# The second product of a seven-product matrix step adds onto the first one's PSUM bank, and the last 128 output rows leave in one transfer

## The chip, the core and the metric

The kernel runs on one core of a Trainium2 chip. A core has TensorE (PE, with its weight loads listed apart as PEld), VectorE (DVE), ScalarE (ACT), GpSimd (POOL) and SyncE (SP, which here only issues DMA transfers). Each engine works through its own list of instructions in order; waits on semaphores tie the lists together. The metric is the device time of one execution in microseconds (us), as the median of several runs.

## What is computed

Attention with rotary positions (2 batches, 8 heads, 576 tokens, head size 64) gives `x` of 1152 tokens by 512. On it runs a dense mixture of four experts, and this layer alone is touched by the change:

```python
p = domain_probs / (domain_probs.sum(-1, keepdims=True) + 1e-09)
for e in range(E):                       # E = 4
    h = np.maximum(x @ w1[e], 0.0)       # 512 -> 1024
    out += p[:, e:e + 1] * (h @ w2[e])   # 1024 -> 512
```

## The kernel before

Every operand of a matmul is split into a high and a low part in fp32r, so a product is three matmuls: high by high, high by low, low by high. The tokens are cut in two chunks. Chunk 0 (512 tokens of the first batch) goes through the experts while the second batch's attention runs. Chunk 1 (640 tokens) goes through them at the end, alone, and this is where the change lies: class `Moe1`, lines 721 to 850.

**First layer of chunk 1** (`first_layer`, lines 804 to 830). For each expert `e` the 1024 hidden columns are cut into four blocks `i` of 256. A block is a 2 by 2 matrix product done with seven half-size products instead of eight (the Winograd form of Strassen). `product` (line 748) issues one of them: six matmuls of 320 columns into one PSUM bank (lines 758 to 761), then the work on the result. For p1 that is a copy to SBUF on ACT (line 766). p2, p4, p5 and p3 each end a quarter of the hidden layer in `hidden` (line 791): an add in place in the bank on DVE (lines 788, 789), the ReLU into the high part on ACT (line 797), and the low part on DVE (line 799), which is queued behind the next product's DVE work. p6 and p7 and p5 also make the running sums `u` and `v` with one DVE add each. p1's copy is read twice: by p6's add and by p2's add. For expert 0 the order is p1 of all four blocks, p2 of all four blocks, and then p6, p7, p5, p4, p3 block by block. For experts 1 to 3 it is p1, p6, p7, p5, p2, p4, p3 block by block.

**Banks.** There are eight PSUM banks, taken in turn (`bank`, line 740). Expert 0's p1 takes banks 4 to 7; the next four, taken ahead at line 737, are those of its p2.

**Second layer** (`second_layer`, lines 836 to 850). Eight steps `f` of five token tiles `t`, three matmuls of 512 columns each (lines 844 to 846) into five banks. In the last step each tile's bank is mixed into `acc` on DVE (`mix`, line 627; the instruction is at line 633). After the last expert `acc` leaves: tiles 0 to 3 on SP's queue (line 639), tile 4, which holds the last 64 rows of both batches, as two transfers of 64 rows, one on SP's and one on ACT's queue (lines 641 to 644).

**Weights** (`Weights`, lines 481 to 548). `load` issues one DMA of 512 KB on SP; `split` makes the high part on ACT (line 136) and the low part on POOL (line 143); for the first-layer weights of experts 1 to 3 it first makes four sums and differences on DVE (line 538) and splits those too. `next` is a load and a split. In the first layer of experts 1 to 3 it is called after each p4, in the second layer after every second step, the last one behind the mixes.

**Quarters** (lines 646 to 711) prepares the token side of the seven products: sums of quarters of `x` (lines 666, 671) and their split (line 678 on ACT, line 682). Its last five steps stand in the program just before chunk 1's first product, and expert 0's p1 copies stand behind them on ACT.

The order of the instructions is the order of the program; nothing reorders it.

Of the kernel before, what the change touches and what calls it, by code (L numbers as in the profile page):

```python
# [56 lines left out]
def kernel(  # L57
# [17 lines left out]
    nc = tc.nc  # L75
    B, H, S, D = q.shape
    NT, DM = out.shape
    E, _, FF = w1.shape
# [3 lines left out]
    SM = NR * P  # L82
    ST = S - SM
# [7 lines left out]
    NF = FF // P  # L91
    FB = 2

    def f32(ap):
        return ap.bitcast(F32)
# [15 lines left out]
    TH = ctok[1] // 2  # L111
# [34 lines left out]
    class Pair:  # L146


        def __init__(self, b, hp, pool, dst, tail_dst):
            self.b, self.hp, self.nm = b, hp, f"{b}_{hp}"  # L150
            self.pool = pool
            self.dst, self.tail_dst = dst, tail_dst
            self.raw, self.hl, self.tp, self.tl, self.tr = ({} for _ in range(5))
            self.sc, self.mx, self.e, self.et, self.seg = ({} for _ in range(5))
# [394 lines left out]
    class Moe:  # L549
# [77 lines left out]
        def mix(self, e, t, po):  # L627
            p = probs[:, t + self.c * NR, e : e + 1]
            acc = self.acc[t]
            if e == 0:  # L630
                nc.vector.tensor_scalar_mul(acc, po, p)
            else:
                nc.vector.scalar_tensor_tensor(  # L633
                    out=acc, in0=po, scalar=p, in1=acc, op0=ALU.mult, op1=ALU.add
                )
            if e == E - 1:
                if t < NR:
                    rows = out[self.c * S : self.c * S + SM, :].rearrange("(p r) d -> p r d", r=NR)
                    nc.sync.dma_start(out=rows[:, t, :], in_=acc)
                else:  # L640
                    for b in range(B):
                        (nc.sync, nc.scalar)[b].dma_start(
                            out=out[b * S + SM : (b + 1) * S, :], in_=acc[b * ST : (b + 1) * ST]
                        )

    class Quarters:

# [73 lines left out]
    class Moe1(Moe):  # L721
# [3 lines left out]
            p1=("a11", "x00"), p2=("a12", "x10"), p3=("s3", "x11"), p4=("a22", "t4"), p5=("s0", "t1"),  # L725
# [3 lines left out]
        def __init__(self, ctx, quarters):  # L729
            self.c, self.n, self.quarters = 1, ctok[1], quarters  # L730
            tilewise = dict(reuse_waits="tile")
            self.h = ctx.enter_context(tc.tile_pool(name="h1", bufs=1, **tilewise))
            self.pp = ctx.enter_context(tc.tile_pool(name="pm1", bufs=1, space=PSUM, **tilewise))
            self.acc = [
                self.h.tile([P, DM], F32, tag=f"acc{i}", name=f"acc1_{i}") for i in range(self.n // P)
            ]
            self.used, self.ahead = 4, [self.bank(f"p2_{i}", i) for i in range(4)]
            self.x, self.lows = {}, []

        def bank(self, name, i=None):  # L740
# [7 lines left out]
        def product(self, e, i, p):  # L748

            w, x = self.TERMS[p]  # L750
            if w[0] == "a":
                f, d = int(w[1]) - 1, int(w[2]) - 1
                ws = [y[:, 2 * d : 2 * d + 2, f * P : (f + 1) * P] for y in wts.got[1, e, 0, i]]
            else:
                ws = [y[:, int(w[1])] for y in wts.sums[e, i]]
            (wh, wl), (xh, xl) = ws, self.quarters.operand(x)
            o = self.bank(f"{p}{e}_{i}")[:, 0:TH]
            for j in range(2):
                nc.tensor.matmul(o, lhsT=wh[:, j], rhs=xh[:, j], start=(j == 0), stop=False)  # L759
                nc.tensor.matmul(o, lhsT=wh[:, j], rhs=xl[:, j], start=False, stop=False)  # L760
                nc.tensor.matmul(o, lhsT=wl[:, j], rhs=xh[:, j], start=False, stop=(j == 1))  # L761
            x, lows = self.x, self.lows
            self.lows = []
            if p == "p1":
                x["p1", i] = self.temp("p1", e, i, NF // FB)
                nc.scalar.activation(out=x["p1", i], in_=o, func=AF.Copy)
            elif p == "p6":
                x["u", i] = self.temp("u", e, i)
                self.add(x["u", i], o, x["p1", i])
            elif p == "p7":  # L770
                x["v", i] = self.temp("v", e, i)
                self.add(x["v", i], o, x["u", i])
            elif p == "p5":
                self.add(x["u", i], o, x["u", i])
                self.hidden(e, 2 * i + 1, 1, o, x["v", i])
            elif p == "p2":
                self.hidden(e, 2 * i, 0, o, x["p1", i])
            elif p == "p4":
                self.hidden(e, 2 * i + 1, 0, o, x["v", i])
            elif p == "p3":  # L780
                self.hidden(e, 2 * i, 1, o, x["u", i])
            for f in lows:
                f()
# [4 lines left out]
        def add(self, out, o, x):  # L788
            nc.vector.tensor_tensor(out=out, in0=o, in1=x, op=ALU.add)  # L789

        def hidden(self, e, f, t, o, other):

            if f not in self.hh:
                self.hh[f] = [self.h.tile([P, self.n], F32R, tag=f"h{x}{f}", name=f"h{x}1_{e}_{f}") for x in "HL"]
            hi, lo = (x[:, t * TH : (t + 1) * TH] for x in self.hh[f])
            self.add(o, o, other)
            nc.scalar.activation(out=hi, in_=o, func=AF.Relu)  # L797
            self.lows.append(
                lambda: nc.vector.scalar_tensor_tensor(  # L799
                    out=lo, in0=o, scalar=0.0, in1=f32(hi), op0=ALU.max, op1=ALU.subtract  # L800
                )
            )

        def first_layer(self, e):

            nb = NF // FB
            self.hh = {}
            if e == 0:
                for i in range(nb):
                    self.product(e, i, "p1")  # L810
                wts.next()
                for i in range(nb):
                    self.product(e, i, "p2")
                wts.load()
                wts.split()
                wts.load()
            for i in range(nb):
                for p in ("p6", "p7", "p5", "p4", "p3") if e == 0 else ("p1", "p6", "p7", "p5", "p2", "p4", "p3"):
                    self.product(e, i, p)
                    if p == "p4" and e:  # L820
                        wts.next()
                if e == 0:
                    wts.split()
                    if i == 2:
                        wts.split()
                    elif i < 2:
                        wts.load()
            for f in self.lows:
                f()
            self.lows = []  # L830
# [5 lines left out]
        def second_layer(self, e):  # L836
            n = self.n
            po = [self.bank(f"po1_{e}_{t}") for t in range(n // P)]
            for f in range(NF):
                fb, fi = divmod(f, FB)  # L840
                wH, wL = (w[:, fi, :] for w in wts.got[1, e, 1, fb])
                for t in range(n // P):
                    sH, sL = (x[:, t * P : (t + 1) * P] for x in self.hh[f])
                    nc.tensor.matmul(po[t], lhsT=sH, rhs=wH, start=(f == 0), stop=False)  # L844
                    nc.tensor.matmul(po[t], lhsT=sH, rhs=wL, start=False, stop=False)  # L845
                    nc.tensor.matmul(po[t], lhsT=sL, rhs=wH, start=False, stop=(f == NF - 1))  # L846
                    if f == NF - 1:
                        self.mix(e, t, po[t])
                if fi == FB - 1:
                    wts.next()  # L850

    class Agenda:
# [153 lines left out]
    for hp, pr in enumerate(first):  # L1006
# [3 lines left out]
        if hp + 1 < NP:  # L1010
            nx, t = first[hp + 1], TURNS[min(hp, 2)]
# [135 lines left out]
```

## Time and profile before

| | us |
|---|---|
| median of 3 runs | 568.88 |
| lowest and highest run | 568.68, 569.23 |
| profiled execution | 566.62 |
| its span, first to last instruction | 564.8 |

The rows come from the profiled execution; its times count from the start of its span. An execution has 1.8 us outside the span. Chunk 1's four experts fill the span from 348.9 us on.

### The profile page before, as it was taken

To read this page: it belongs to the slowest core of one execution; us is meant where nothing else is said; L and a number is where in the kernel's file an instruction comes from. 1 tells how busy PE (TensorE), PEld (TensorE's weight loads), DVE (VectorE), ACT (ScalarE), POOL (GpSimd) and SP (SyncE) were. 2 spreads that over 40 slices of the span, in tenths; PEclk is the share of its full clock that TensorE was granted. 3 is DMA by queue.
4 is the path that set the end of the run, shared out by engine and by line. 5 is a ranking of instruction groups with operands and counts; after the bars stand their busy time and mean duration, and the time that the engine had idled before them with its cause. 6 is when DMAs were issued, how large, how long until landed. Compare 5 with 4: busy or idle time off the path is not lost. (4 is left out here: it accounts for less than half of the span.)

```text
span 564.8 us, 8507 instructions
## 1 busy us (share of the span) xinstructions
PE 539.7 (96%) x3157; PEld 474.3 (84%) x3157; DVE 324.0 (57%) x587; ACT 281.0 (50%) x561; POOL 339.3 (60%) x240
## 2 busy tenths in 40 slices
PE   4898998999999999999999999999999999999996
PEld 3787887788888888888888888888898899889985
DVE  5588897244363534453344546994587668757702
ACT  5688888555444545555545553453344234324400
POOL 7999984558715871487433487458554655565400
PEclk9899999999999999999999999999999999999999
DMA  5245023352234123432142214522223213222102
GB/s 153 71 117 145 17 51 99 81 173 93 77 113 140 41 76 102 131 97 64 62 128 74 62 52 150 185 76 74 77 77 111 74 39 113 78 76 85 61 1 93
DMA packets 48732, 50.68 MB, mean 90 GB/s; under 512 B 15538, under 2 KB 38322, under 8 KB 48690
## 3 DMA queue, kind: packets, MB, share of 16 engines
q1 hardware_dynamic: 47890, 49.38, 29.0%
q10 hardware_dynamic: 800, 0.75, 0.5%
q8 instruction: 25, 0.41, 0.3%
q14 instruction: 17, 0.14, 0.1%
HBM read 43.34 MB, written 2.36 MB: 81 GB/s over the span
## 5 line engine op out<-in xcount | busy, mean ns | idle before, releaser
L143 POOL TENSOR_TENSOR wl<-wr,wh 128x1024 fp32r<-128x1024 f32 x64 | 154.4, 2413 | 136.0 <-ACT wh L136 136.0
L136 ACT ACTIVATE wh<-wr 128x1024 fp32r<-128x1024 f32 x64 | 67.2, 1052 | 26.5 <-PE po L600 11.9
L300 DVE TENSOR_REDUCE mx<-sc 128x1 f32<-128x576 f32 x72 | 54.2, 753 | 37.7 <-PE sc L289 37.0
L143 POOL TENSOR_TENSOR sl<-sf,sh 128x1024 fp32r<-128x1024 f32 x16 | 38.5, 2407 | 43.0 <-ACT sh L136 43.0
L846 PE MATMUL po<-wh,hL 128*128 128x512 f32 x160 | 62.3, 389 | 0.0
L845 PE MATMUL po<-wl,hH 128*128 128x512 f32 x160 | 62.3, 389 | 0.0
L844 PE MATMUL po<-wh,hH 128*128 128x512 f32 x160 | 62.3, 389 | 0.0
L308 ACT ACTIVATE e<-sc,mx 128x576 f32<-128x576 f32 x72 | 53.3, 740 | 17.7 <-DVE mx L300 16.7
L584 DVE SCALAR_TENSOR_TENSOR hL<-ph,hH 128x512 fp32r<-128x512 f32 x32 | 22.1, 692 | 60.1 <-ACT hH L583 60.1
L598 PE MATMUL po<-wh,hH 128*128 128x512 f32 x128 | 52.3, 409 | 0.0
L136 ACT ACTIVATE sh<-sf 128x1024 fp32r<-128x1024 f32 x16 | 17.0, 1060 | 70.5 <-DVE sf L538 64.9
L623 PE MATMUL ph<-xH,wh 128*128 128x512 f32 x128 | 51.5, 402 | 0.0
L624 PE MATMUL ph<-xL,wh 128*128 128x512 f32 x128 | 50.1, 392 | 0.4 <-POOL xL L424 0.4
L343 DVE TENSOR_TENSOR ptL<-pp,ptH 128x512 fp32r<-128x512 f32 x64 | 44.0, 687 | 11.1 <-ACT ptH L339 10.3
L339 ACT ACTIVATE ptH<-pp 128x512 fp32r<-128x512 f32 x64 | 38.1, 595 | 24.6 <-PE x L372 17.3
L600 PE MATMUL po<-wh,hL 128*128 128x512 f32 x128 | 50.3, 393 | 0.0
L625 PE MATMUL ph<-xH,wl 128*128 128x512 f32 x128 | 50.1, 392 | 0.0
L599 PE MATMUL po<-wl,hH 128*128 128x512 f32 x128 | 50.0, 391 | 0.0
L797 ACT ACTIVATE hH<-p 128x320 fp32r<-128x320 f32 x64 | 27.1, 436 | 40.3 <-DVE p L789 40.3
L322 PE MATMUL pp<-ident,e 128*128 128x128 f32 x288 | 44.7, 279 | 2.1 <-DVE ptL L343 1.1
L538 DVE TENSOR_TENSOR sf<-wr 128x256 f32<-128x256 f32 x30 | 32.7, 1129 | 16.9 <-DMA wr<-in_moe_w_dram 16.9
L322 PEld LDWEIGHTS pp<-ident,e 128*128 128x128 f32 x288 | 34.2, 142 | 8.1 <-ACT e L308 2.4
(171 smaller groups left out, 1373.4 us busy)
## 6 DMA issues: line engine op xcount, KB each, us to landing
wr<-in_moe_w_dram SPq DMA_DIRECT2D x68, 512.0 KB, 3.6
k2T<-kT SPq DMA_DIRECT2D x14, 288.0 KB, 4.1
rawv<-in_v_dram SPq DMA_DIRECT2D x16, 128.0 KB, 3.0
out_dram<-acc SPq DMA_DIRECT2D x8, 256.0 KB, 4.0
rawk<-in_k_dram SPq DMA_DIRECT2D x7, 256.0 KB, 3.8
rawq<-in_q_dram SPq DMA_DIRECT2D x7, 256.0 KB, 3.1
rawv<-in_v_dram SPq DMA_DIRECT2D x16, 32.0 KB, 2.3
tabs<-in_rope_dram ACTq DMA_DIRECT2D x1, 320.0 KB, 3.4
```

The lines of the kernel that those rows point to most:

```text
L136: nc.scalar.activation(out=hi, in_=src, func=AF.Copy)
L143: eng_l.tensor_tensor(out=lo, in0=src, in1=f32(hi), op=ALU.subtract)
L300: nc.vector.tensor_reduce(out=mx, in_=self.sc[u][:, :, 0:HALF], op=ALU.max, axis=AX.XY, negate=True)
L308: nc.scalar.activation(out=e.rearrange("p (i c) -> p i c", i=2), in_=self.sc.pop(u)[:, :, 0:HALF], func=AF.Exp, bias=self.mx.pop(u), accum ...
L322: nc.tensor.transpose(pp[:, c * P : (c + 1) * P], self.e[u][:, c * P : (c + 1) * P], ident)
L598: nc.tensor.matmul(po[t], lhsT=sH, rhs=wH, start=(f == 0), stop=False)
L600: nc.tensor.matmul(po[t], lhsT=sL, rhs=wH, start=False, stop=(f == NF - 1))
L623: nc.tensor.matmul(o, lhsT=wH[:, kt], rhs=xh, start=(kt == 0), stop=False)
L624: nc.tensor.matmul(o, lhsT=wH[:, kt], rhs=xl, start=False, stop=False)
L844: nc.tensor.matmul(po[t], lhsT=sH, rhs=wH, start=(f == 0), stop=False)
L845: nc.tensor.matmul(po[t], lhsT=sH, rhs=wL, start=False, stop=False)
L846: nc.tensor.matmul(po[t], lhsT=sL, rhs=wH, start=False, stop=(f == NF - 1))
```

## The change

p2's six matmuls accumulate onto p1's bank, after p1's copy has been read from it by ACT, so p2's sum is complete in PSUM and its add on DVE is gone; the copy stays for p6. A block uses six banks instead of seven, and the four banks taken ahead go to the first four products behind p2. The last `next` of a second layer moves to behind the first p1 of the next expert. Tile 4 of the output leaves in one transfer of 128 rows on ACT's queue.

```diff
@@ mix
-                    for b in range(B):
-                        (nc.sync, nc.scalar)[b].dma_start(
-                            out=out[b * S + SM : (b + 1) * S, :], in_=acc[b * ST : (b + 1) * ST]
-                        )
+                    nc.scalar.dma_start(out=out.rearrange("(b s) d -> b s d", s=S)[:, SM:S, :], in_=acc)
@@ Moe1.__init__
-            self.used, self.ahead = 4, [self.bank(f"p2_{i}", i) for i in range(4)]
+            self.used, self.ahead = 4, [self.bank(f"p6_{i}", i) for i in range(4)]
@@ product
-            o = self.bank(f"{p}{e}_{i}")[:, 0:TH]
+            onto = p == "p2"
+            o = self.x.pop(("p1 sum", i)) if onto else self.bank(f"{p}{e}_{i}")[:, 0:TH]
+            group = dict(skip_group_check=True) if p in ("p1", "p2") else {}
             for j in range(2):
-                nc.tensor.matmul(o, lhsT=wh[:, j], rhs=xh[:, j], start=(j == 0), stop=False)
-                nc.tensor.matmul(o, lhsT=wh[:, j], rhs=xl[:, j], start=False, stop=False)
-                nc.tensor.matmul(o, lhsT=wl[:, j], rhs=xh[:, j], start=False, stop=(j == 1))
+                nc.tensor.matmul(o, lhsT=wh[:, j], rhs=xh[:, j], start=(j == 0 and not onto), stop=False, **group)
+                nc.tensor.matmul(o, lhsT=wh[:, j], rhs=xl[:, j], start=False, stop=False, **group)
+                nc.tensor.matmul(o, lhsT=wl[:, j], rhs=xh[:, j], start=False, stop=(j == 1), **group)
             if p == "p1":
+                x["p1 sum", i] = o
                 x["p1", i] = self.temp("p1", e, i, NF // FB)
                 nc.scalar.activation(out=x["p1", i], in_=o, func=AF.Copy)
...
             elif p == "p2":
-                self.hidden(e, 2 * i, 0, o, x["p1", i])
+                self.hidden(e, 2 * i, 0, o)
@@ hidden
-        def hidden(self, e, f, t, o, other):
+        def hidden(self, e, f, t, o, other=None):
...
-            self.add(o, o, other)
+            if other is not None:
+                self.add(o, o, other)
@@ first_layer
-                    if p == "p4" and e:
+                    if e and (p == "p4" or i == 0 and p == "p1"):
                         wts.next()
@@ second_layer
-                if fi == FB - 1:
+                if fi == FB - 1 and f < NF - 1:
                     wts.next()
```

## Rows read from the trace of the kernel before

**Rows 1.** Page, part 1: busy us, share of the span, instructions of each engine.

```profile
PE 539.7 (96%) x3157; PEld 474.3 (84%) x3157; DVE 324.0 (57%) x587; ACT 281.0 (50%) x561; POOL 339.3 (60%) x240
```

**Rows 2.** Windows by stage: length, busy us (instructions) per engine, PEclk, DMA share, GB/s.

```profile
348.00:377.00 29.00, 27.09 (x174) 25.43 (x173) 27.34 (x59) 13.11 (x26) 15.30 (x9) 1.00 0.47 162
377.00:404.20 27.20, 27.20 (x121) 22.51 (x121) 15.51 (x26) 10.07 (x13) 21.25 (x9) 1.00 0.24 78
404.20:429.00 24.80, 24.80 (x170) 24.79 (x169) 19.34 (x45) 11.79 (x23) 12.38 (x6) 1.00 0.28 87
...
533.00:561.00 28.00, 26.95 (x119) 21.96 (x117) 5.37 (x10) 1.71 (x3) 2.40 (x1) 1.00 0.08 28
```

**Rows 3.** Timeline of PE, expert 0's first layer: start, us, instruction, [idle before <-releaser].

```profile
352.29 0.31 PE L761 MATMUL p<-xH,wl 128*128 128x320 f32 x1
...
356.18 0.31 PE L761 MATMUL p<-xH,wl 128*128 128x320 f32 x1
356.83 0.41 PE L759 MATMUL p<-tH,sh 128*128 128x320 f32 x1 [0.34 <-ACT p L766]
...
364.38 0.42 PE L759 MATMUL p<-t1H,sh 128*128 128x320 f32 x1 [0.49 <-DVE hL L799]
...
369.84 0.41 PE L759 MATMUL p<-t1H,sh 128*128 128x320 f32 x1 [0.78 <-DVE hL L799]
...
376.98 0.39 PE L844 MATMUL po<-wh,hH 128*128 128x512 f32 x1
```

**Rows 4.** Timeline of ACT around the first copies of p1.

```profile
352.37 0.81 ACT L678 ACTIVATE tH<-s 128x320 fp32r<-128x320 f32 x2
355.84 0.47 ACT L678 ACTIVATE tH<-s 128x320 fp32r<-128x320 f32 x1 [2.65 <-DVE s L671]
356.34 1.43 ACT L766 ACTIVATE p<-p 128x320 f32<-128x320 f32 x4
```

**Rows 5.** Timeline of DVE in the same layer: two of p2's adds, p6's first add.

```profile
358.40 0.89 DVE L789 TENSOR_TENSOR p<-p,p 128x320 f32<-128x320 f32 x2
...
363.45 0.48 DVE L789 TENSOR_TENSOR u<-p,p 128x320 f32<-128x320 f32 x1
```

**Rows 6.** Timeline of ACT in expert 1's first layer: copies of p1, blocks 0 and 1.

```profile
408.57 0.42 ACT L766 ACTIVATE p<-p 128x320 f32<-128x320 f32 x1
...
414.14 0.44 ACT L766 ACTIVATE p<-p 128x320 f32<-128x320 f32 x1
```

**Rows 7.** Timeline of the end: last matmul, the last transfer on ACT's queue.

```profile
559.56 0.39 PE L846 MATMUL po<-wh,hL 128*128 128x512 f32 x1
...
560.77 0.55 ACTq L642 DMA_DIRECT2D out_dram<-acc  x1
```

**Rows 8.** Line 642, its two transfers of 128 KB: issue to landing.

```profile
DMA to landing us min/median/max: 2.4/2.7/3.0
```

**Rows 9.** Windows of the end, columns as in rows 2.

```profile
558.90:559.60 0.70, 0.70 (x5) 0.55 (x3) 0.70 (x2) 0.00 (x0) 0.00 (x0) 1.00 0.98 366
...
563.20:563.50 0.30, 0.00 (x0) 0.00 (x0) 0.00 (x0) 0.00 (x0) 0.00 (x0) 1.00 0.07 27
```

**Rows 10.** Tile `probs`, line 122: the transfer that loads the same 128 rows' probabilities.

```profile
L122 SPq DMA_DIRECT2D probs<-in_moe_domain_probs_dram x1: 647/647/647, 19.8 to 19.8; - x1
```

**Rows 11.** Window while that transfer moves, columns as in rows 2.

```profile
21.40:21.50 0.10, 0.10 (x3) 0.10 (x1) 0.10 (x1) 0.10 (x2) 0.10 (x1) 0.98 0.19 5
```

**Rows 12.** Windows at three changes of the granted clock, columns as in rows 2.

```profile
17.50:18.00 0.50, 0.11 (x2) 0.00 (x0) 0.00 (x0) 0.50 (x2) 0.50 (x1) 0.99 0.25 57
18.00:18.50 0.50, 0.00 (x0) 0.00 (x0) 0.00 (x0) 0.50 (x3) 0.50 (x2) 0.50 0.51 160
...
21.00:21.50 0.50, 0.50 (x4) 0.50 (x3) 0.47 (x2) 0.50 (x2) 0.41 (x2) 0.60 0.07 2
...
564.00:564.20 0.20, 0.00 (x0) 0.00 (x0) 0.00 (x0) 0.00 (x0) 0.00 (x0) 0.81 0.00 0
```

**Rows 13.** Timeline of PE around the first of these falls.

```profile
16.62 0.53 PE L238 MATMUL tpq<-identr,hlq 128*128 128x128 f32 x4 [0.80 <-POOL hlq L143]
...
18.56 0.85 PE L289 MATMUL sc<-kT,qT 128*128 128x288 f32 x2 [0.95 <-ACT e L308]
```

## The prediction, made before the changed kernel was run

> **What bounds the kernel now.** I read the page first: PE is busy for 96% of the span [rows 1], so only its idle time and what lies before its first and behind its last matmul can move the end. Then the windows by stage [rows 2]. From 377 us on PE has no gap: the second layer of expert 0 fills 27.20 of 27.20 us, the first layer of expert 1 fills 24.80 of 24.80, and experts 2 and 3 look the same, up to the last matmul at 559.56 us [rows 7]. Work taken off DVE there (19.34 busy of 24.80) is worth nothing. The one stage with gaps is expert 0's first layer: 27.09 of 29.00 us. Its price per matmul I take from expert 1, where nothing waits: 168 matmuls (4 blocks, 7 products, 6 matmuls) in 24.8 us, 0.1476 us each. Expert 0's 168 should so take 24.8 us. They start at 352.29 - 23 x 0.1476 = 348.9 and end at 376.98 [rows 3], 28.1 us: 3.3 us of gaps, in front of the products behind p2, with ACT's p1 copy and DVE's low parts as releasers. So the timeline of PE there is the next view, and those of ACT and DVE beside it [rows 4, 5]. Last comes the tail: from 559.56 us to the end of the span 5.3 us pass, in which only output leaves.
>
> **Part 1, p2 onto p1's bank, expert 0.** What goes: p2's four adds, two of them in 0.89 us [rows 5], some 1.7 us of DVE. What comes: p2's first matmul, which in the kernel before went into a bank of its own, has to wait until ACT has copied p1's sum out of the bank that it now adds to. That copy is late. ACT works in order; ahead of the four copies stands a split of Quarters that waits 2.65 us for DVE until 355.84, and the copies run from 356.34 on, four in 1.43 us [rows 4]. Nothing in the change touches what they wait for. PE is done with p1's 24 matmuls at 352.4 and went straight on into p2, up to 356.18 [rows 3]; now it finds nothing to do until the first copy is out. That very event has a row: p6's first matmul takes the bank of the first p1 before, was released by the copy and started at 356.83 [rows 3]. So p2 starts at 356.83, and queued behind it on PE are 4 + 20 products, 144 matmuls: 144 x 0.1476 = 21.25 us, with 0.1 us for the first matmul behind a wait (0.41 instead of 0.31 us), to 378.2 us. That stands against 376.98: **+1.2 us**, if all later gaps are gone.
>
> Are they? They came from banks which DVE released late: p5's first matmul of the second block waited for a low part until 364.38, that of the third until 369.84 [rows 3]. DVE began p6's adds at 363.45, 5.7 us behind p6's end near 357.7. In the changed kernel p2 ends at 360.4, its ReLUs and low parts by about 361, the weight sums follow, and p6's first add comes at about 362.7: DVE is 0.7 us earlier, PE 3.6 us later. Walking the eight banks with 0.4 us per DVE instruction and 0.88 us per product, the tightest place, p5 of the third block at 370.9 on the bank of p3 of the first, finds it free at 369.1. I take 0 for later gaps; if DVE is late by what it was, 0.5 to 1 us comes on top.
>
> **Part 2, what the wait does to the clock.** The wait leaves PE without work from 352.6 to 356.8, some 4.1 us; the longest gap that PE has in the trace once its work has begun is 0.95 us [rows 13]. Two rows show the granted clock fall from 2.4 to 1.2 GHz: at 18.0 us, after PE had worked only in pieces with gaps of 0.80 and 0.95 us [rows 12, 13], and at 564.1, 4.2 us after the end of the last matmul at 559.95 [rows 7, 12]. At 18.0 far less idleness was enough than here, so I expect a fall during this wait or just behind it. Price: the first fall lasted to about 21.4 (the half-microsecond to 21.5 has 0.60), with PE at work again from 18.56: 2.8 us at half the clock [rows 12, 13], of which half is lost, **+1.4 us**. The ends are 0 (no fall) and 2.8 us (the low clock lasts twice as long). PE paces this stage afterwards, so the loss goes into the end in full.
>
> The Trainium skill, page "TensorE: Matmul & The Clock Gate", section "Why this matters for your kernels", speaks against this part: gaps between bursts of matmuls send the clock back to the low level. By it the sum is the one with the fall, without it the second case below. The trace agrees as far as it goes: it has a fall 4.2 us behind the last matmul [rows 7, 12].
>
> **Part 3, experts 1 to 3.** Twelve adds go, PE has no gap that they could close: 0. Does the new wait bite? p2 is fifth in its block, so it wants p1's copy 4 x 0.885 = 3.5 us behind the block's start. In expert 1's block 0 (start 404.2) the copy ran at 408.57 [rows 6], too late for a p2 at 407.7. But it ran there behind the splits that the change now puts behind it: p1 ends at 405.3, so the copy ends by 405.8. Block 1's copy ended at 414.58 [rows 6] where p2 will start at 404.2 + 6.2 + 3.5 = 413.9; p6's first add, which waited for block 0's copy, starts some 2.4 us earlier now, so DVE and ACT come to block 1 without that lag, and the copy follows p1's end at 411.5. Cost 0, with 0.7 us for each block after the first as the other end, if the lag stays.
>
> The moved `next`: its load keeps its place among SP's loads, as nothing else is on that queue between; its four sums keep theirs on DVE, as p1 has no DVE work; on ACT two splits now stand behind p1's copy, and with them POOL's two. Their product is block 3 of the next expert's first layer, wanted 18.5 us later: 0. With six banks a block, p7 of the next block takes the bank of p2: it starts at 7.9 us in block time, p2's low part ends near 6.4. Cost 0 with 1.5 us of cover.
>
> **Part 4, the last transfer.** Before, 256 KB left as two transfers issued at 560.77 [rows 7], which landed 2.4 and 3.0 us later [rows 8]. Their data were out by 563.2 [rows 9], and the first could not start before about 561.9, 1.1 us after issue, with the four earlier tiles ahead of it: 1.3 us for the data. The new one has the form of line 122 [rows 10]: the last 64 rows of two batches as an outer dimension of two. While that one moved, the DMA share was 0.19 and 5 GB/s [rows 11], at most 3 of 16 engines' time, where output of 128 plain rows has 0.98 and 366 GB/s [rows 9]; it is also the only transfer here without a landing shown. So I expect that the outer two is spread over two engines. An engine's pace from [rows 9] is 366 / (0.98 x 16) = 23.3 GB/s. 262,144 bytes on two engines take 5.6 us, on three 3.7, on sixteen 0.7. I take two, since there are two outer rows: 5.6 instead of 1.3 us, **+4.3 us**, nothing behind it to hide it. The other end is all sixteen, where the tail saves what the SP transfer was later than ACT's, up to 0.6 us.
>
> The Trainium skill, page "DMA: Bandwidth & Descriptors", section "Why a DMA increments its semaphore by 16 and not by 1", says that a transfer uses the largest number of engines up to 16 which divides the slowest dimension of both its patterns. That gives 2 here and 16 for the two transfers of 64 rows. The row of line 122 agrees in direction (0.19 of the engines). Without the rule the sum would be that of the third case below.
>
> **Sum.** 1.2 + 1.4 + 4.3 = 6.9 us. On the profiled execution: span 564.8 to 571.7, execution 566.62 to 573.5. The median of the runs is 2.3 us above the profiled one; on it the forecast is 568.88 + 6.9 = **575.8 us**.
>
> **The rivals.**
> - *The clock holds* over the wait: 568.88 + 5.5 = 574.4. For it: the gap before the fall at the end was as long, so the fall might come too late to matter. Against: the fall at 18.0. Chance 0.2.
> - *The transfer spreads over sixteen engines* as the others do: 575.8 - 4.3 - 0.3 = 571.2, or 569.8 if the clock holds too. For it: line 122 is a load of 2 KB and tells little of a store of 256 KB. Chance 0.12.
> - *The freed DVE pays*, the other side: the copies of p1 are out before PE wants p2, all 3.3 us of gaps close and the tail is neutral: 565.6. It decides from copies that end by 352.4 on; each microsecond later costs one, and at 355.7 nothing is left. The copies' row ends 356.8 to 357.8. Chance 0.04, in which a slow tail would leave 569.9, about the time of now.
> - *The lag in experts 1 to 3 stays*: 0.7 us for each of 9 blocks, up to 6.3 us: 577 to 582. For it: block 1's row. Against: both causes of the lag are removed. Chance 0.08.
>
> **How the numbers follow.** The forecast has 0.56. Its own bounds: part 1 +1.0 to +2.2, the clock 0.6 to 2.8, the tail 3.7 to 4.5, so about 574.2 to 578.4. With the held clock (down to 573.4) and the lower part of the lag (to 578.8) the range is 573.2 to 578.8 and leaves the sixteen engines, the freed DVE and the upper half of the lag outside, 0.2. About 0.2% is what a measurement of this kernel can tell from no change, 567.7 to 570.0. Faster: 0.03. Same: 0.04, from part of the sixteen engines with the clock held and of the freed DVE. Slower: 0.93.
>
> **What would show it.** Part 1: a PE gap of about 4 us in front of line 759's first p2, released by ACT's p1 copy, the second layer's start at 378 to 380, and no gap by DVE's low parts behind it. Part 2: PEclk of 0.50 within 355 to 362 us. Part 3: first layers of 24.8 us without idle PE. Part 4: a landing of some 7 us, and a DMA share near 0.12 to 0.19 in the last microseconds. The forecast is wrong if ACT's copies run before 355 us, or if the last transfer lands within 3 us.

## The result: 1.4% slower, and where the time went

The changed kernel takes 577.25 us (median of 6 runs, 575.05 to 578.14) against 568.84 us for the kernel before in the same runs: ratio 1.0142, 95% interval 1.0122 to 1.0163, so 6.9 to 9.3 us more. The profiled execution took 577.79 us, its span is 576.0 us. The page of after, which answers to [rows 1], with the slices of the granted clock:

```profile
span 576.0 us, 8485 instructions
...
PE 543.6 (94%) x3157; PEld 478.5 (83%) x3157; DVE 319.0 (55%) x571; ACT 280.7 (49%) x561; POOL 338.9 (59%) x240
...
PEclk9999999999999999999999999899999999999997
```

The 16 adds are gone from DVE (571 instead of 587 instructions). PE's busy time rose although it does the same matmuls: part of them ran at a lower clock. Windows by stage are the next view (columns as in [rows 2]): expert 0's first layer, then everything up to the last matmul, then the tail. First the kernel before, cut at its own stage limits, then after.

```profile
348.92:376.98 28.06, 26.16 (x169) 24.66 (x168) 26.47 (x58) 13.09 (x26) 14.38 (x8) 1.00 0.45 156
376.98:559.95 182.97, 182.97 (x986) 163.81 (x984) 113.70 (x209) 62.63 (x103) 94.03 (x39) 1.00 0.22 72
559.95:564.83 4.88, 0.00 (x1) 0.00 (x0) 0.79 (x2) 0.00 (x0) 0.00 (x0) 0.93 0.59 190
```

```profile
350.92:382.67 31.75, 27.57 (x169) 27.30 (x168) 27.56 (x59) 15.58 (x28) 15.81 (x9) 0.89 0.50 155
382.67:565.64 182.97, 182.97 (x986) 163.80 (x984) 106.46 (x191) 59.81 (x100) 92.34 (x39) 1.00 0.22 69
565.64:576.00 10.36, 0.00 (x1) 0.00 (x0) 0.79 (x2) 0.00 (x0) 0.00 (x0) 0.69 0.26 90
```

Three things are to be seen. The middle, 183 us with three of the four experts, is the same to the hundredth, with 7 us less of DVE in it. Expert 0's first layer is 3.7 us longer, the tail 5.5 us. Together 9.2 us; the spans differ by 11.2. The other 2.0 us lie ahead of 348.92 and 350.92, where both programs are the same: this start varies from run to run, and in the traces it goes with how long the granted clock is low in the opening. In the four traces in which chunk 1 begins by 349.2 us the low level ends by 21.6 us (in before at 21.4 [rows 12]); in the nine others it lasts past 22 us. That this is the whole 2.0 us is argued, not shown. The same two matmuls of both runs on the timeline of PE, before at the high level and then after at the low one:

```profile
14.91 0.53 PE L289 MATMUL sc<-kT,qT 128*128 128x288 f32 x2 [0.42 <-ACT e L308]
```

```profile
14.88 0.85 PE L289 MATMUL sc<-kT,qT 128*128 128x288 f32 x2 [0.41 <-ACT e L308]
```

In all the kernels below chunk 1 began between 348.9 and 351.3 us. So stages are compared by their length, and times by their ratio.

**Expert 0's first layer.** Timelines of PE and of ACT in after, answering to [rows 3, 4]:

```profile
354.28 0.31 PE L760 MATMUL p<-xH,wl 128*128 128x320 f32 x1
358.78 0.64 PE L758 MATMUL p<-xH,wh 128*128 128x320 f32 x1 [4.18 <-ACT p L766]
359.21 0.47 PE L759 MATMUL p<-xL,wh 128*128 128x320 f32 x1
...
382.67 0.39 PE L845 MATMUL po<-wh,hH 128*128 128x512 f32 x1
```

```profile
357.79 0.47 ACT L675 ACTIVATE tH<-s 128x320 fp32r<-128x320 f32 x1 [2.61 <-DVE s L668]
358.29 1.42 ACT L766 ACTIVATE p<-p 128x320 f32<-128x320 f32 x4
```

p2's first matmul waits 4.18 us for p1's copy, which stands on ACT behind the split that waits for DVE. That is the only gap that PE has from here to the end; the gaps in front of the later products [rows 3] are gone. But behind the wait a matmul takes 0.47 us instead of 0.31. Windows behind the wait:

```profile
358.78:364.75 5.97, 5.97 (x22) 5.97 (x23) 2.90 (x8) 3.19 (x7) 2.38 (x1) 0.50 0.40 150
364.75:382.67 17.92, 17.92 (x123) 17.92 (x123) 16.95 (x42) 9.65 (x16) 8.72 (x4) 1.00 0.31 89
```

The granted clock is at 0.50 for 5.97 us of PE's work. In that time PE did 22 matmuls; at 0.1476 us each they take 3.2 us at full clock. So some 2.7 us went to the clock and 1.0 us to the wait itself.

**The tail.** The last transfer's issue, SP's last wait before and in after, and three windows of after while the transfer is alone:

```profile
566.47 1.12 ACTq L641 DMA_DIRECT2D out_dram<-acc  x1
```

```profile
SPq L1142 <- DMA out_dram<-acc: 2.4, 1, 2.4
```

```profile
SPq L1143 <- DMA out_dram<-acc: 8.8, 1, 8.8
```

```profile
569.00:570.00 1.00, 0.00 (x0) 0.00 (x0) 0.00 (x0) 0.00 (x0) 0.00 (x0) 0.78 0.15 27
570.00:571.00 1.00, 0.00 (x0) 0.00 (x0) 0.00 (x0) 0.00 (x0) 0.00 (x0) 0.50 0.11 43
571.00:572.00 1.00, 0.00 (x0) 0.00 (x0) 0.00 (x0) 0.00 (x0) 0.00 (x0) 0.50 0.14 55
```

SP waited 8.8 us at the end for the output, 2.4 us before the change. The mean busy share of the sixteen DMA engines is 0.11 to 0.15, as if two of sixteen worked (0.125), with 27 GB/s at first and 43 to 55 later. The packets in the trace say the same: from 568 us on, two packets of 2 KB are under way at a time. The Trainium skill, page "DMA: Bandwidth & Descriptors", section "Why a DMA increments its semaphore by 16 and not by 1", says that a transfer runs on the largest number of engines, up to 16, that divides the slowest dimension of both its patterns, here two. The trace agrees with its two packets at a time.

### The profile page after: what moved, and what is told of

Its sections match the earlier page's. It is cut to its first block, busy times and chain, and to the rows that moved or that the text cites. A ratio compares the mean times of both kernels' runs of the same rounds, so it can differ in the third digit from the quotient of the medians.

```text
span 576.0 us, 8485 instructions
## 1 busy us (share of the span) xinstructions
PE 543.6 (94%) x3157; PEld 478.5 (83%) x3157; DVE 319.0 (55%) x571; ACT 280.7 (49%) x561; POOL 338.9 (59%) x240
```

## The experiments

"First layer" is expert 0's, from its first matmul to the second layer's first; "tail" runs from the end of the last matmul to the end of the span. Both are from the profiled execution of each kernel. Each ratio is against the kernel before as run beside that kernel, with medians of 568.00 to 568.84 us; e5 and e11 rest on two runs each. The stretch between them was 182.97 us in every one of these kernels.

| kernel | first layer | tail | median, us | ratio to before (95%) |
|---|---|---|---|---|
| before | 28.06 | 4.88 | 568.84 | |
| after | 31.75 | 10.36 | 577.25 | 1.0142 (1.0122 to 1.0163) |
| e1_two_transfers | 31.36 | 4.70 | 571.92 | 1.0067 (1.0042 to 1.0092) |
| e2_tail_alone | 28.07 | 10.38 | 572.93 | 1.0094 (1.0062 to 1.0126) |
| e3_filled_wait | 29.13 | 4.90 | 568.72 | 1.0014 (0.9997 to 1.0032) |
| e4_copies_first | 28.03 | 4.69 | 568.29 | 1.0001 (0.9986 to 1.0016) |
| e5_one_on_sp | 28.08 | 9.71 | 572.68 | 1.0083 (1.0053 to 1.0113) |
| e6_two_on_act | 28.08 | 5.36 | 569.11 | 1.0011 (0.9997 to 1.0026) |
| e7_experts_1_to_3 | 28.07 | 4.86 | 568.60 | 1.0003 (0.9992 to 1.0015) |
| e9_ve_relieved | 28.20 | 4.89 | 568.90 | 1.0011 (0.9998 to 1.0024) |
| e10_sums_behind | 27.53 | 4.87 | 568.09 | 1.0000 (0.9985 to 1.0015) |
| e11_column_halves | 28.07 | 10.74 | 573.43 | 1.0097 (1.0059 to 1.0136) |
| e12_sums_ahead | 26.34 | 4.90 | 566.90 | 0.9963 (0.9949 to 0.9976) |

**The two parts of the change, each alone.** e1 is the changed kernel with the two transfers of before; e2 is the kernel before with the one transfer.

```diff
  e1, against after
-                    nc.scalar.dma_start(out=out.rearrange("(b s) d -> b s d", s=S)[:, SM:S, :], in_=acc)
+                    for b in range(B):
+                        (nc.sync, nc.scalar)[b].dma_start(
+                            out=out[b * S + SM : (b + 1) * S, :], in_=acc[b * ST : (b + 1) * ST]
+                        )
  e2, against before: the same lines the other way round
```

> The changed kernel with the last 128 rows sent as before, 64 rows on each of two queues. Theory (the two parts of the change cost separately: 5.5 us in the tail, some 3 us by p2's wait and the clock behind it): 571.7 us, 2.9 above the kernel before; the tail from the last matmul to the end of the span is 4.9 us again; the gap of 4.2 us in front of p2 stays. Rival (the transfer is slow because of something earlier in the changed kernel, not by its form): the tail stays near 10 us and the time near 577.

> The kernel before with nothing but the one transfer of 128 rows on ScalarE's queue. Theory (its form puts it on two of the engines): 568.8 + 5.5 = 574.3 us, tail some 10 us, PE's work as before. Rival (a transfer of 256 KB on one queue costs as others do): 568 to 569 us.

Measured: e1 has the tail of before and the long first layer, e2 the reverse; 1.0067 and 1.0094 make 1.016, the changed kernel has 1.0142. So the parts add up within their intervals. e2's 572.93 us lie 1.4 under what was expected, while its tail of 10.38 us is what was expected; the runs' starts vary by as much.

**What makes the transfer slow: queue, bytes or form?** e5 puts the one transfer on SP's queue, e6 puts both transfers of 64 rows on ACT's, e11 sends two transfers of the new form, each with half of the columns, on the two queues.

```diff
  e5, against e2
-                    nc.scalar.dma_start(
+                    nc.sync.dma_start(
  e6, against before
-                        (nc.sync, nc.scalar)[b].dma_start(
+                        nc.scalar.dma_start(
  e11, against e2
+                    for i in range(2):
+                        a, z = i * DM // 2, (i + 1) * DM // 2
+                        (nc.sync, nc.scalar)[i].dma_start(
+                            out=out.rearrange("(b s) d -> b s d", s=S)[:, SM:S, a:z], in_=acc[:, a:z]
+                        )
```

> The kernel before with the one transfer of 128 rows on SyncE's queue in place of ScalarE's. Theory (the outer dimension of two puts it on two engines, whatever the queue): tail 10 us or more, DMA share near 0.13 while it moves, 573 to 575 us. Rival (ScalarE's queue is what is slow): tail 5 us, 568.8 us.

> The kernel before with both transfers of 64 rows on ScalarE's queue. Theory (the form decides, not the queue or the number of bytes on it): tail within 0.7 us of the kernel before, 568.5 to 569.5 us. Rival (256 KB on one queue behind each other are slow): tail 8 us or more.

> The kernel before with the last 128 rows as two transfers that each have the outer dimension of two and half of the columns, one on SyncE's and one on ScalarE's queue. Theory (an outer dimension of two means two engines, the same two for each transfer): tail about 10 us as with one transfer, DMA share near 0.13, 573 us. Rival (each transfer gets two engines of its own): the data take half as long, tail near 7.5 us, DMA share near 0.25.

Measured: on SP the tail is 9.71 us, a little under the 10 us expected, so 0.7 us of it go with the queue. Two of the old form behind each other on ACT cost 0.5 us, not 5. Windows during the transfer in e5 and then in e11, where two transfers of the new form run at once:

```profile
566.00:567.00 1.00, 0.00 (x0) 0.00 (x0) 0.00 (x0) 0.00 (x0) 0.00 (x0) 0.50 0.13 51
```

```profile
568.00:569.00 1.00, 0.00 (x0) 0.00 (x0) 0.00 (x0) 0.00 (x0) 0.00 (x0) 0.50 0.14 47
569.00:570.00 1.00, 0.00 (x0) 0.00 (x0) 0.00 (x0) 0.00 (x0) 0.00 (x0) 0.50 0.13 47
```

Two such transfers on two queues together still have 0.13 to 0.14 of the engines and two packets under way at a time: they share the same two. So the form decides, and splitting such a transfer over queues doesn't help.

**Is the clock a cost of its own?** e3 is e1 with work for PE during the wait.

```diff
  e3, against e1
+        def fill(self, e, i):
+            wh = wts.got[1, e, 0, i][0][:, 0:2, 0:P]
+            xh = self.quarters.operand("x00")[0]
+            o = self.ahead[i][:, 0:TH]
+            for j in range(6):
+                nc.tensor.matmul(o, lhsT=wh[:, j % 2], rhs=xh[:, j % 2], start=(j == 0), stop=(j == 5))
...
+                for i in range(nb):
+                    self.fill(e, i)
                 for i in range(nb):
                     self.product(e, i, "p2")
```

> As e1, and in front of expert 0's first p2 stand 24 matmuls of 320 columns onto the four banks that p6 to p4 of the first block take later; nobody reads their sums. p2 still waits for p1's copy, but PE works meanwhile. Theory (the wait costs 1.2 us by itself and the rest of the 3 us is the clock that falls over it): PEclk stays at 1.0 over this layer, 570.0 us, 1.7 below e1. Rival (the clock's fall is paid by slack that DVE would have taken anyway): the time of e1, 571.7 us.

Timeline of PE and two windows of e3 during and behind the wait:

```profile
353.82 4.06 PE L813 MATMUL p<-xH,wh 128*128 128x320 f32 x24
358.21 0.42 PE L761 MATMUL p<-xH,wh 128*128 128x320 f32 x1 [0.33 <-ACT p L769]
```

```profile
355.00:358.00 3.00, 2.88 (x18) 2.61 (x18) 2.97 (x5) 0.76 (x2) 1.31 (x1) 1.00 0.97 364
358.00:361.00 3.00, 2.79 (x19) 2.79 (x20) 1.83 (x5) 2.19 (x6) 0.00 (x0) 1.00 0.41 126
```

p2 still starts when the copy is out, but at clock 1.00. The first layer takes 29.13 us, 2.2 less than e1, where the low clock covered 5.1 us of PE's work: that is the clock's price. What is left over before, 1.07 us, is the wait's. The time fell further than expected, to 568.72 us instead of 570.0; of the 3.2 us between the medians of e1 and e3 the layer accounts for 2.2, the rest is not resolved. Twenty-four useless matmuls make the kernel faster than nothing in their place.

**Experts 1 to 3.** e7 is e1 with the accumulation in these experts only.

```diff
  e7, against e1
-            onto = p == "p2"
+            onto = p == "p2" and e > 0
-                self.hidden(e, 2 * i, 0, o)
+                self.hidden(e, 2 * i, 0, o, None if onto else x["p1", i])
```

> As e1, but only experts 1 to 3 add p2 onto p1's bank; expert 0 has its own banks and the add for p2, as in the kernel before. Theory (PE has no gap in experts 1 to 3 either way, and p1's copy there comes before PE wants p2): 568.7 us, no PE gap in these experts, the first layer of expert 0 takes 28.1 us again. Rival (the copies come late there too, up to 0.7 us a block): 571 to 575 us.

Measured: no difference to the kernel before (0.9992 to 1.0015), and 182.97 us of gapless PE. Twelve fewer DVE adds are worth nothing there, and accumulating onto a bank that ACT has read costs nothing either.

**If the copy came in time, would the freed DVE pay?** e4 is e1 with the last steps of Quarters behind p1's products, so that ACT has the copies first.

```diff
  e4, against e1
                     self.product(e, i, "p1")
+                for _ in range(5):
+                    quarter_step()
                 wts.next()
...
-        for _ in range(5):
-            quarter_step()
```

> As e1, with the last five steps of the quarters moved behind expert 0's four p1 products, so that on ScalarE p1's copies stand ahead of the split that waits for VectorE. Theory (p2's cost is the late copy, nothing in the accumulation itself): no gap of 4 us, PEclk 1.0, the first layer of expert 0 ends some 2 us earlier than in the kernel before, 566.5 us. Rival (adding onto a bank that another engine has just read is slow, or VectorE's late start holds the layer anyway): 568.8 us or more.

Half of this came: p2 waits 0.36 us and the clock stays at 1.00. But the layer takes 28.03 us, as before, not 26. PE, DVE and POOL in e4:

```profile
354.50 0.42 PE L761 MATMUL p<-xH,wh 128*128 128x320 f32 x1 [0.36 <-ACT p L769]
...
365.90 0.42 PE L761 MATMUL p<-t1H,sh 128*128 128x320 f32 x1 [0.48 <-DVE hL L803]
371.35 0.42 PE L761 MATMUL p<-t1H,sh 128*128 128x320 f32 x1 [0.79 <-DVE hL L803]
```

```profile
361.52 1.29 DVE L803 SCALAR_TENSOR_TENSOR hL<-p,hH 128x320 fp32r<-128x320 f32 x3 [1.51 <-ACT hH L801]
362.72 1.52 DVE L538 TENSOR_TENSOR sf<-wr 128x256 f32<-128x256 f32 x2
...
364.96 0.48 DVE L792 TENSOR_TENSOR u<-p,p 128x320 f32<-128x320 f32 x1
```

```profile
361.24 2.39 POOL L143 TENSOR_TENSOR sl<-sf,sh 128x1024 fp32r<-128x1024 f32 x1 [4.78 <-ACT sh L136]
```

p6's first add comes 364.96 - 350.46 = 14.5 us after the layer's start; before the change it was 363.45 - 348.92 = 14.5 [rows 5]. The 1.6 us of adds that were taken out turned into waiting: DVE waits 1.51 us instead of 0.70 for p2's ReLUs, which stand on ACT behind a split, and a pair of sums takes 1.52 us instead of 0.75. The wait, one of the adds and the same pair in the kernel before, on DVE, and then POOL:

```profile
359.99 0.49 DVE L799 SCALAR_TENSOR_TENSOR hL<-p,hH 128x320 fp32r<-128x320 f32 x1 [0.70 <-ACT hH L797]
360.40 0.49 DVE L789 TENSOR_TENSOR p<-p,p 128x320 f32<-128x320 f32 x1
...
361.99 0.75 DVE L538 TENSOR_TENSOR sf<-wr 128x256 f32<-128x256 f32 x2
```

```profile
359.71 2.40 POOL L143 TENSOR_TENSOR sl<-sf,sh 128x1024 fp32r<-128x1024 f32 x1 [4.77 <-ACT sh L136]
```

There the sums begin as POOL's subtraction ends (362.1), and take 0.75 us; the add, with one operand in PSUM, took its usual 0.49 us beside POOL. In e4 the sums begin in the middle of POOL's subtraction: the first of the pair alone takes 1.19 us and ends 0.3 us behind POOL's instruction, the second takes its usual 0.41 us. So DVE's sums stand still while POOL works, and the adds of before had filled time in which the sums would have stood still anyway.

e9 was made before I had seen this: it moves the second block's sums to POOL and the splits behind p2.

```diff
  e9, against e4
-                (nc.vector if e or fb else nc.gpsimd).tensor_tensor(out=x[:, o], in0=p, in1=q, op=op)
+                (nc.vector if e or fb > 1 else nc.gpsimd).tensor_tensor(out=x[:, o], in0=p, in1=q, op=op)
-                wts.next()
                 for i in range(nb):
                     self.product(e, i, "p2")
+                wts.next()
```

> As e4, and two things that take the load off VectorE before p6: the weight sums of the second block of expert 0 run on GpSimd instead of VectorE, and the load and split that stood between p1 and p2 stands behind p2, so that p2's ReLUs on ScalarE don't stand behind a split. Theory (in e4 the freed adds of VectorE turned into waiting for these ReLUs, and VectorE holds the layer): p6's first add comes 3 to 4 us earlier against the layer's start than the 14.5 us of the kernel before, the layer takes 26 to 27 us instead of 28.1, and the time is 567 to 567.5 us. Rival (the low part of the second block's sums, later on GpSimd, takes the place of VectorE): a wait for it in front of p6 of the second block, 28 us, 568.7 us.

Neither theory had it. The layer takes 28.20 us and p6's first add comes at 363.69 - 349.02 = 14.7 us. DVE and POOL of e9:

```profile
356.24 2.91 DVE L682 TENSOR_TENSOR tL<-s,tH 128x320 fp32r<-128x320 f32 x3
359.07 1.27 DVE L803 SCALAR_TENSOR_TENSOR hL<-p,hH 128x320 fp32r<-128x320 f32 x3
360.27 2.71 DVE L538 TENSOR_TENSOR sf<-wr 128x256 f32<-128x256 f32 x2
```

```profile
354.97 1.95 POOL L538 TENSOR_TENSOR sf<-wr 128x256 f32<-128x256 f32 x2
356.89 0.97 POOL L538 TENSOR_TENSOR sf<-sf,wr 128x256 f32<-128x256 f32 x1
357.94 0.86 POOL L538 TENSOR_TENSOR sf<-wr,sf 128x256 f32<-128x256 f32 x1
359.97 2.39 POOL L143 TENSOR_TENSOR sl<-sf,sh 128x1024 fp32r<-128x1024 f32 x1 [1.17 <-ACT sh L136]
```

With POOL at work three low parts of the quarters (`tL`) take 2.91 us (1.29 in e4 and e10, where POOL rests), and a pair of sums 2.71 us instead of 0.75. What POOL took over DVE lost again. The Trainium skill, page "SBUF — State Buffer", section "Who interferes with whom", says that a VectorE instruction with two inputs in SBUF contends with a GpSimd instruction that reads SBUF, and one with at most one such input does not. The traces agree on both: sums and low parts of `s` against the adds from PSUM.

e10 and e12 test this by order alone. e10 keeps all sums on DVE and puts them ahead of POOL's subtraction, behind p2; e12 puts them ahead of p2's work as well, with the splits still behind p2's ReLUs.

```diff
  e10, against e4
-                wts.next()
                 for i in range(nb):
                     self.product(e, i, "p2")
+                wts.next()
  e12, against e10: the sums split off from the splits
+                wts.load()
+                wts.ahead(2)       # the sums of the next two blocks
                 for i in range(nb):
                     self.product(e, i, "p2")
-                wts.next()
+                wts.split()
```

> As e4, but the weight sums and splits of expert 0's second and third block stand together behind p2's four products; all sums stay on VectorE. Theory (in e4 and e9 VectorE's sums of the third block stood still under GpSimd's 2.4 us subtraction for the second block, in which the kernel before had its adds; here both sums come ahead of that subtraction): p6's first add comes 12 to 13 us after the layer's start instead of 14.5, no sum takes over 0.6 us by more than one instruction, and the next that is late is the second block's low part from GpSimd, 1.5 to 2 us in front of p6 of the second block; the layer takes 27 to 27.7 us. Rival (VectorE's own amount of work sets 14.5 us): 14 us or more, layer 28 us.

> As e10, but VectorE makes the sums of expert 0's second and third block ahead of p2's work, while the splits of these sums on ScalarE and GpSimd stay behind p2's ReLUs. Theory (the layer is held by the chain of VectorE's sums, ScalarE's high part and GpSimd's low part in front of p6 of the second block): GpSimd's low part comes 1.4 us earlier against the layer's start, the gap of 1.97 us of e10 shrinks to about 0.6 us, the layer takes 26.1 to 26.5 us instead of the 28.1 us of the kernel before, and the time is 566.3 us against 568.2, about 0.3% less. Rival (VectorE, with its low parts later, holds the banks): a gap in front of p5 of the second block as in the kernel before, layer 27.5 us or more.

PE, DVE and POOL of e10, then of e12:

```profile
364.57 0.42 PE L763 MATMUL p<-tH,sl 128*128 128x320 f32 x1 [1.97 <-POOL sl L143]
...
362.21 0.48 DVE L792 TENSOR_TENSOR u<-p,p 128x320 f32<-128x320 f32 x1
...
362.06 4.82 POOL L143 TENSOR_TENSOR sl<-sf,sh 128x1024 fp32r<-128x1024 f32 x2 [5.97 <-ACT sh L136]
```

```profile
364.25 0.41 PE L772 MATMUL p<-tH,sl 128*128 128x320 f32 x1 [0.41 <-POOL sl L143]
...
360.39 0.75 DVE L551 TENSOR_TENSOR sf<-wr 128x256 f32<-128x256 f32 x2
...
363.05 0.48 DVE L801 TENSOR_TENSOR u<-p,p 128x320 f32<-128x320 f32 x1
...
361.70 4.86 POOL L143 TENSOR_TENSOR sl<-sf,sh 128x1024 fp32r<-128x1024 f32 x2 [4.78 <-ACT sh L136]
```

In e10 p6's first add comes 362.21 - 350.06 = 12.2 us after the layer's start, the sums run unhindered, and PE now waits once, 1.97 us, for POOL's low part: 27.53 us, within the expected bounds, though too little for the time to show it. In e12 that low part starts 361.70 - 350.90 = 10.8 us after the layer's start instead of 12.0, PE waits 0.41 us, and the layer takes 26.34 us. e12 is faster than both kernels: 0.9963 (0.9949 to 0.9976) of the kernel before. It has the accumulation, the two transfers of before, the copies first and the sums first. No run has the new order without the accumulation, so how its gain divides between the two is not shown.

## Why the prediction held, step by step

Forecast 575.8 us in a range of 573.2 to 578.8; measured 577.25, and 8.1 us by the ratio where the sum was 6.9.

- **What bounds the kernel:** right. The stretch behind expert 0's first layer did not move, 182.97 us in all kernels.
- **Part 1, the wait:** right. Released by the event that had released p6, 4.18 us long (forecast 4.1), the only gap in the layer, 1.07 us net by e3 (forecast 1.2). No later gap, as the walk over the banks had it, in e3 at full clock either.
- **Part 2, the clock:** mechanism right, size off. Forecast 1.4, measured 2.2 (e1 against e3) to 2.7 (in after). The length of the low clock was taken from one early row, 2.8 us of PE's work [rows 12, 13]; here it was 5.1 in e1 and 5.97 in after. The upper end, 2.8, held. One row of a state that begins and ends at moments of its own is a sample, not a duration.
- **Part 3:** right. No cost and no gain (e7).
- **Part 4, the tail:** mechanism right, size off: forecast 4.3 with bounds of 3.7 to 4.5, measured 5.5. Two engines did carry it, and from 570 us on at about the forecast 23.3 GB/s an engine (43 to 55 GB/s for both). But the transfer starts slowly, with 27 GB/s from 569 to 570 us, so its data took 6.8 us, from the first packet at 567.74 to the end of the last at 574.51, instead of 5.6. The longer issue, 1.12 us instead of 0.55 [rows 7], is not the cause: the first packet comes 1.27 us behind the start of the issue, and 1.21 us before the change. Why the transfer starts slowly is open. The total stayed in the range because the other parts lie within their bounds.
- **The rivals:** the clock that holds fell by after's PEclk, the sixteen engines by e2 and e5, the lag in experts 1 to 3 by e7. The rival on the other side was priced wrongly: it promised 3.3 us from the copies' being early, and e4 gave it that and gained nothing. I had read the gaps as DVE's amount of work. They came from a chain, DVE's sums, ACT's split, POOL's subtraction, DVE's next sums, in which the adds lay under cover of POOL. The new order on top of less work took 1.7 us off the layer (e12); less work with the copies early took nothing off (e4), and the order without the accumulation was not run.

## What to carry to other kernels

An accumulation that saves an engine an add puts a wait on TensorE for whoever still reads the bank; look at what that reader is queued behind, and add the clock that falls over the gap to the gap itself. Joining two transfers into one is no gain if the joined form has a short outer dimension: two rows of outer dimension were two of sixteen engines. Before an engine is relieved, see whether the work taken out was filling time in which its next instruction could not run.

## What was not expected of the hardware

- DVE instructions with two SBUF operands stretch up to the end of POOL's instruction: a pair of sums took 0.75 us with POOL at rest, 1.52 (e4) and 2.71 us (e9) beside POOL's 2.4 us subtraction, while adds with a PSUM operand kept their 0.49 us.
- Two transfers with an outer dimension of two, on different queues, shared the same two engines (e11): 0.13 of the sixteen, two packets under way and 47 GB/s for both together, as for one.
- After a gap of 4.2 us the clock stayed low for 5.97 us of dense work (5.1 in e1); 24 matmuls whose sums nobody reads were worth 2.2 us (e3).
